# Modulation rows by column parts in the opening of an S4 convolution and SwiGLU kernel

## Chip, core and metric

The kernel runs on one core of a Trainium2 chip. The metric is the device time of one execution in microseconds, the median of several runs. TensorE (PE) multiplies, VectorE (DVE), ScalarE (ACT) and GpSimd (POOL) work on tiles of 128 partitions, SyncE (SP) issues transfers.

## Reference

```python
def _A_ref(u, A_re, A_im, B_re, B_im, C_re, C_im, log_dt, Dskip):
    dt = jnp.exp(log_dt)[:, None]
    ...
    P = jnp.exp(logdA[:, :, None] * l[None, None, :])
    K = jnp.einsum("dn,dnl,dn->dl", Cc, P, dB).real
    ...
    y = ... + u * Dskip[None, None, :]      # causal convolution of u with K, by FFT

def _B_ref(x, w_gate, w_up, w_down):
    g = _silu(x @ w_gate)
    u = x @ w_up
    return (g * u) @ w_down

x = A_u                                      # 1 x 2048 x 448
mod = (_silu(c) @ w_mod).reshape(c.shape[0], 6, 1, -1)
sa, ca, ga, sb, cb, gb = (mod[:, 0], mod[:, 1], mod[:, 2], mod[:, 3], mod[:, 4], mod[:, 5])
h = _layernorm(x, axis=-1) * (1 + ca) + sa
x = x + ga * _A_ref(h, ...)
h = _layernorm(x, axis=-1) * (1 + cb) + sb
x = x + gb * _B_ref(h, ...)                  # F = 1792
```

A condition vector c gives six rows of 448 values: a shift, a scale and a gate for each of two branches (groups 0 to 5 of `w_mod`). The first branch is a causal convolution over the 2048 tokens, the second a gated feed-forward.

## The kernel before

The 2048 tokens are 16 tiles of 128; blocks of 2, 2, 3, 3, 3 and 3 tiles pass through the feed-forward one after another (`run_blocks`). In a block, `gate_up` multiplies the block's transposed, normed rows by a column strip of both weights (line 703), split into a high and a low part (`hhi`, `hlo`, `gu`) so that one-pass products keep the precision; Silu (ACT, 718), a multiply (DVE, 731) and a split into `phi` and `plo` (734, 735) follow, and `down` multiplies the last strip but one by its down-weights (747). The next block's convolution and norm run between.

With the sizes of the states here the convolution kernel K is nearly linear in time, and the kernel takes it as K0 - slope, two rows `k0` and `k1`, if a flag that it computes allows it (`flag_sum`, `flag_of`; another path stands in the program otherwise). A convolution is then a product with a triangle of ones plus running sums of the tiles before (`run0`, `run1`).

The opening (lines 257 to 481) prepares all that for the first two tiles:

- SP loads states, x and the modulation weights in the order of `ORDER` ("sc": a state, "m10": group 1, first half, "w0": a strip of gate_up, "d0": of down, "x2": a tile of x).
- The steps run in the order of `PLAN`, a hand-set list of names out of the table `todo` (lines 434 to 481). Each engine executes its own instructions in this order, and each waits for what it needs.
- A modulation row (`mod_part`, 237 and 241): the columns of silu(c) are spread over 128 columns as the stationary operand, and five products sum in one bank, so that all 128 partitions hold the row: 1+ca and sa (groups 1, 0), the branch gate ga (group 2), 1+cb (4), sb (3), and gb (5, in two parts, `end_gate`).
- K's sums are columns (channel on the partition): `total` on ACT, `slope` on DVE. `row_of` (354) spreads such a column to a row in four products with the identity. The gate ga is then multiplied into `k0`, `k1` and the spread Dskip (`gd`).
- Convolution of the two tiles (437): `o00` to `o14`; the skip `hd` and x itself enter through products with the identity (322, 437).
- Norm (`st`, `r`, `n1`, `n2`), turning to channels (`to_channels`, 403), `hhi` and `hlo` (408, 413). The shift sb is added as a row ahead of the turn; as columns (`sbc`, for the later blocks) it is turned by line 373.
- The running rows after tile 1 come from three full and fast products with `left` (393) and go to partition 0 by `left_sbuf` (397).
- The weights of the first strips are split by ACT (116, 124) and DVE or POOL (118, 126, 128).

In the main loop the running rows are made on partitions 96 to 127, and a transfer that ACT issues brings the last of them to partition 0 (930 to 932).

Of the kernel before, what the change touches and what calls it, by code (L numbers as in the profile page):

```python
# [40 lines left out]
ORDER = """sf x0 x1 sc m10 se m11 sd m20 m21 m00 sb m01 sa m40 m41 d0 w0 m30 m31 m50 w2 d1 x2 w1 x3 d2 m51"""  # L41

PLAN = """t1 t4 pa0 t2 pa1 pg0 pg1 t3 S1 ca h00 S2 ps0 wr wi ps1 a2 m0 t5 a3 sq1 k0 cb0 S3 ga cb1 w0 h01 gd h11 m1 k1 gm0 h10
hd0 sb0 gm1 hd1 gc1 v00 v10 gc0 o00 o01 sq0 o02 o10 v01 sa w02 d10 o13 st0 r0 o12 cbr v11 d11 o11 o14 sb1 n10 w2 w01
st1 r1 d00 sbr e0 n11 n20 du0 tr0 n21 hi0 du1 tr1 l0 fs l1 sbt lo00 hi1 w1 lo10 fl lo01 sbc x1 e1 lo11 w11 w21 x0 eg
w22 lc w12 d01"""
# [6 lines left out]
def f32(ap):  # L53
    return ap.bitcast(F32)
# [3 lines left out]
def tile_kernel(ctx, tc, x, a_re, a_im, b_re, b_im, c_re, c_im, log_dt, dskip,  # L58
# [172 lines left out]
    cs = const.tile([128, 5], F32)  # L231

# [11 lines left out]
    def end_gate(ks):  # L244

        mod_part(CV, m5.rearrange("p a b -> p (a b)"), ks)
# [9 lines left out]
    with tc.tile_pool(name="pre", bufs=1) as pre:  # L256
        vec = pre.tile([128, 8], F32)
        sc.dma_start(vec, vecs)
        drow = pre.tile([1, D], F32)
        sc.dma_start(drow, dskip.rearrange("(o d) -> o d", o=1))  # L260
# [30 lines left out]
        all1 = pre.tile([128, 128], F32)  # L291
# [6 lines left out]


        left = pre.tile([128, 3, 33], F32R)  # L300
        left_ = pre.tile([128, 3, 33], F32)
        po.memset(left_, 0.0)
        po.memset(left_[:, 0, 0:1], 1.0)
        for q in range(2):
            po.memset(left_[:, 1 + q, 32:33], 1.0)
            po.tensor_scalar(left_[:, 1 + q, 0:1], tok, -1.0, 256.0 - 128.0 * q, op0=OP.mult, op1=OP.add)
        po.tensor_copy(left, left_)
# [13 lines left out]
        for q in range(2):  # L321
            pe.matmul(os[q], ident, xs[q], start=True, stop=False)
        pd = bank()[:, 0:D]
        pe.matmul(pd, all1[0:1, :], drow, start=True, stop=True)
        sc.copy(gd, pd)
# [11 lines left out]
                               (("h", F32, D), ("v0", F32, D), ("v1", F32R, D), ("hd", F32, D), ("h2", F32, 512)))  # L337
        sbr = pre.tile([128, 512], F32)
        ga = pre.tile([128, D], F32)
        t_, WV = f32(tri), po  # L340

        def part(t, k):
            return t[:, k * N:min((k + 1) * N, NS_)]
# [700 lines left out]
```

## Time and profile before

| | us |
|---|---|
| median of 3 runs | 490.55 (489.42 to 490.78) |
| the profiled execution | 488.68 |
| its span, first to last instruction | 486.9 |
| TensorE busy | 477.3 |
| DVE, ACT, POOL busy | 283.2, 155.0, 61.8 |
| start of line 703 | 38.64 |
| first product of line 747 | 43.81 |
| mean granted TensorE clock | 0.998 |

A row of a timeline gives the start from the span's first instruction, the time until the end of the last of the instructions that the row merges, the engine (a q behind it: its queue, which issues or waits), the line and operation, what it writes and reads, the shape and the number of records. A bracket gives idle time of the engine ahead of the row and what ended it. A full-precision product is shown as two records.

### The profile page before, as it was taken

What the parts mean: (1) busy time and instruction counts of PE and PEld (TensorE: products, weight loads), DVE (VectorE), ACT (ScalarE), POOL (GpSimd) and SP (SyncE); (2) the same over time, 40 slices, a digit from 0 to 9 for tenths busy, and PEclk for the clock granted to TensorE, in tenths of its full rate; (3) what the DMA queues carried; (4) which work ended last, traced back from release to release, by engine and by line L of the source; (5) the groups of instructions that cost most, each with busy time, mean ns of one, the idle gap of its engine ahead of it and who ended that gap; (6) DMA issues with size and microseconds to landing.
All of it is one profiled execution on the core that took longest, in us unless ns stands there. A gap on an engine that the chain in (4) does not pass through costs nothing.

```text
span 486.9 us, 6980 instructions
## 1 busy us (share of the span) xinstructions
PE 477.3 (98%) x2725; PEld 447.4 (92%) x2725; DVE 283.2 (58%) x543; ACT 155.0 (32%) x338; POOL 61.8 (13%) x86
## 2 busy tenths in 40 slices
PE   8999999999999999999999999999999999999994
PEld 5749988999998999999999999999999999999994
DVE  4868999568886446574644667375475643222134
ACT  5665455522225112332312223231223222221111
POOL 2241001000000040410023221002241000000000
PEclk9999999999999999999999999999999999999999
DMA  8945762020000200101210011130001112000001
GB/s 310 415 161 156 235 193 88 15 96 1 0 3 14 83 1 0 42 30 52 80 44 0 2 43 45 43 114 0 2 0 45 43 44 75 23 1 0 1 0 63
DMA packets 18751, 31.24 MB, mean 64 GB/s; under 512 B 2578, under 2 KB 13460, under 8 KB 18708
## 3 DMA queue, kind: packets, MB, share of 16 engines
q1 hardware_dynamic: 18000, 30.52, 18.3%
q8 instruction: 23, 0.38, 0.3%
q10 hardware_dynamic: 708, 0.19, 0.2%
q14 instruction: 20, 0.16, 0.1%
HBM read 24.61 MB, written 6.03 MB: 63 GB/s over the span
## 4 chain that ended last, share of the span: by engine, by line
PE 94%; DVE 2%; ACT 2%; issue 1%; POOL 0%; DVEq 0%; POOLq 0%; ACTq 0%
PE bank L703 57%; PE dn L747 27%; PE bank L237 2%; PE bank L253 1%; PE dn L437 1%; PE bank L241 1%; ACT raw L196 1%; PE bank L907 1%; PE cv L908 1%; PE cv L906 1%; PE cv L237 0%; PE bank L393 0%; DVE raw L194 0%; PE bank L207 0%; PE bank L920 0%
## 5 line engine op out<-in xcount | busy, mean ns | idle before, releaser
L703 PE MATMUL bank<-hhi,gu 128*128 128x384 f32 (+1 forms) x1169 | 209.4, 318 | 0.0
L703 PEld LDWEIGHTS bank<-hhi,gu 128*128 128x128 f32 x1169 | 189.8, 188 | 3.2 <-issue 0.7
L703 PE MATMUL bank<-hlo,gu 128*128 128x384 f32 (+1 forms) x668 | 130.8, 317 | 0.0
L703 PEld LDWEIGHTS bank<-hlo,gu 128*128 128x128 f32 x668 | 109.2, 188 | 0.0
L731 DVE TENSOR_TENSOR bank<-raw,bank 128x384 f32<-128x384 f32 (+1 forms) x69 | 36.8, 534 | 122.7 <-PE bank L703 120.3
L734 ACT CAST phi<-bank 128x384 fp32r<-128x384 f32 (+1 forms) x83 | 36.9, 445 | 140.8 <-DVE bank L731 140.8
L718 ACT ACTIVATE raw<-bank 128x384 f32<-128x384 f32 (+1 forms) x70 | 32.9, 470 | 121.8 <-PE bank L703 115.3
L735 DVE TENSOR_TENSOR plo<-bank,phi 128x384 fp32r<-128x384 f32 (+1 forms) x83 | 42.5, 512 | 37.6 <-ACT phi L734 37.6
L747 PE MATMUL dn<-wdh,plo 128*128 128x448 f32 x218 | 58.0, 367 | 0.0
L747 PE MATMUL dn<-wdh,phi 128*128 128x448 f32 x218 | 58.0, 367 | 0.0
L747 PE MATMUL dn<-wdl,phi 128*128 128x448 f32 x218 | 57.6, 365 | 0.0
L747 PEld LDWEIGHTS dn<-wdh,plo 128*128 128x128 f32 x218 | 41.0, 188 | 3.6
L747 PEld LDWEIGHTS dn<-wdl,phi 128*128 128x128 f32 x218 | 41.0, 188 | 3.5
L747 PEld LDWEIGHTS dn<-wdh,phi 128*128 128x128 f32 x218 | 38.7, 188 | 1.8 <-ACT run L930 0.7
L168 POOL TENSOR_SCALAR rsb<-mvb 128x1 f32<-128x1 f32 (+2 forms) x13 | 4.7, 360 | 170.6 <-DVE mvb L152 170.6
L168 POOL TENSOR_SCALAR rsa<-mva 128x3 f32<-128x3 f32 (+1 forms) x6 | 1.4, 233 | 118.1 <-DVE mva L152 118.1
L124 ACT CAST gu<-raw 128x1024 fp32r<-128x1024 f32 x14 | 14.6, 1046 | 0.3 <-ACT ga L379 0.3
L881 POOL TENSOR_TENSOR m<-m,gm 128x448 f32<-128x448 f32 x9 | 10.4, 1152 | 21.3 <-DVE m L185 21.3
L895 DVE TENSOR_TENSOR vl<-m,vh 128x448 fp32r<-128x448 f32 x12 | 9.1, 755 | 6.7 <-ACT vh L894 6.1
L237 PE MATMUL bank<-wm,cs 128*128 128x448 f32 x30 | 12.5, 546 | 0.0
L126 DVE TENSOR_TENSOR gu<-raw,gu 128x768 fp32r<-128x768 f32 x13 | 12.3, 950 | 0.0
L118 DVE TENSOR_TENSOR wdl<-rawd,wdh 128x448 fp32r<-128x448 f32 x16 | 9.9, 621 | 3.4 <-ACT wdh L116 3.2
(213 smaller groups left out, 417.8 us busy)
## 6 DMA issues: line engine op xcount, KB each, us to landing
raw<-in_B_w_gate_up_dram SPq DMA_DIRECT2D x14, 512.0 KB, 3.8
rawd<-in_B_w_down_dram SPq DMA_DIRECT2D x16, 224.0 KB, 3.9
x<-in_A_u_dram SPq DMA_DIRECT2D x12, 224.0 KB, 2.9
out_dram<-x SPq DMA_DIRECT2D x11, 224.0 KB, 2.4
xd<-raw SPq DMA_DIRECT2D x9, 256.0 KB, 2.0
raw<-xd SPq DMA_DIRECT2D x36, 64.0 KB, 2.0
wm<-in_w_mod_groups_dram SPq DMA_DIRECT2D x5, 448.0 KB, 8.0
wm<-in_w_mod_groups_dram SPq DMA_DIRECT2D x5, 336.0 KB, 7.9
```

Of the source, the lines that this page charges most:

```text
L118: ve.tensor_tensor(lo, wdn[j], f32(hi), op=OP.subtract)
L124: sc.copy(wgu[j][:, :, 0:4, :], w)
L126: en.tensor_tensor(lo, w[:, :, 0:3, :], f32(hi), op=OP.subtract)
L237: pe.matmul(ps[:, 0:D], cs[:, k:k + 1].to_broadcast([128, 128]), w[:, k * D:(k + 1) * D], start=k == 0, stop=False)
L703: pe.matmul(ps[s][:, 0:n], w[:, s, a], (hlo if lo else hhi)[:, k, 0:n], start=first and q == 0, stop=end and q == len(ka) - 1)
L718: sc.activation(p[:, 0:n], ps[0][:, 0:n], AF.Silu)
L731: ve.tensor_tensor(ps[1][:, 0:n], p[:, 0:n], ps[1][:, 0:n], op=OP.mult)
L734: sc.copy(hi[:, 0:n], ps[1][:, 0:n])
L735: ve.tensor_tensor(lo[:, 0:n], ps[1][:, 0:n], f32(hi[:, 0:n]), op=OP.subtract)
L747: pe.matmul(dn[q][:, 0:D], u[:, cs], v, start=f == 0 and z == 0, stop=f == (NF - 3 if last else NF - 1) and z == 2)
L881: (ve if on_v else po).tensor_tensor(v, h, g, op=OP.mult)
L895: ve.tensor_tensor(vl, v0, f32(vh), op=OP.subtract)
```

## The change

Four of the six modulation rows (groups 2, 4, 3 and 5) are no longer summed in one bank over all partitions. `mod_quads` writes each of the contraction's four parts to its own 32 partitions, with 32 columns of the stationary operand. ACT copies the bank to `qt`, and the sum over the four parts is taken in one of two ways: one product with `pick`, a column that has a one in the first row of each part and is spread over 128 columns (`spread_row`, for 1+cb and gb), or by turning `qt` to columns and summing on DVE (`turned_to`, `columns`, for ga and sb).

The branch gate is so a column `gac`. POOL multiplies it into K's column sums (`scaled`, `gated_dt`) and into Dskip, which now comes with the small vectors as columns (`gdm`) and is spread like K's sums (`gd_row`). Three row multiplies, the copy of the gate's row and its transfer leave the path taken here. sb is added as columns behind the turn (`high`, `low`). The last 64 channels, which need both halves of the partitions, are turned by two products of 64 columns.

Tile 1's x is added by POOL and DVE (`skip`, `branch_1`) in place of two products with the identity, and the running rows after tile 1 come from two fast products with ones into `CV`, a sum on DVE and a transfer that ACT issues (`left_over`, `left_rows`). The small splits of the first strip move from POOL to DVE, and both lists of order are written anew.

```diff
-ORDER = """sf x0 x1 sc m10 se m11 sd m20 m21 m00 sb m01 sa m40 m41 d0 w0 m30 m31 m50 w2 d1 x2 w1 x3 d2 m51"""
...
+ORDER = """sf x0 x1 sc m10 se sd m11 m20 m21 m00 sb m01 sa m40 m41 m30 m31 w0 m50 m51 d0 w1 d1 x2 w2 x3 d2"""
...
+    def mod_quads(ps, w):
+
+        for k in range(3):
+            pe.matmul(ps[32 * k:32 * k + 32, 0:D], cs[:, k:k + 1].to_broadcast([128, 32]), w[:, k * D:(k + 1) * D],
+                      start=True, stop=True)
+        for z in range(2):
+            pe.matmul(ps[96:128, z * D // 2:(z + 1) * D // 2], cs[:, 3 + z:4 + z].to_broadcast([128, 32]), w[:, 3 * D:NM],
+                      start=z == 0, stop=z == 1)
...
+        ve.memset(pick, 0.0)
+        for q in range(4):
+            ve.memset(pick[32 * q:32 * q + 1], 1.0)
...
-        for q in range(2):
-            pe.matmul(os[q], ident, xs[q], start=True, stop=False)
-        pd = bank()[:, 0:D]
-        pe.matmul(pd, all1[0:1, :], drow, start=True, stop=True)
-        sc.copy(gd, pd)
+        pe.matmul(os[0], ident, xs[0], start=True, stop=False)
...
+        def turned_to(ps, t):
+
             for k in range(4):
-                pe.transpose(psm["c"][:, k * 128:(k + 1) * 128], sbr[:, k * 128:(k + 1) * 128], ident)
...
+                o = ps[:, k * 128:(k + 1) * 128]
+                if k < 3:
+                    pe.transpose(o, t[:, k * 128:(k + 1) * 128], ident)
+                else:
+                    for z in range(2):
+                        pe.matmul(o[64 * z:64 * z + 64], t[:, 384:D], ident, start=True, stop=True)
+
+        def columns(to, n):
+            ve.tensor_reduce(to, psm[n].rearrange("p (k a b) -> p k a b", k=4, a=4)[:, :, :, 0], axis=AX.X, op=OP.add)
+
+        def spread_row(n):
+            pe.matmul(psm[n][:, 0:D], pick.to_broadcast([128, 128]), qt[n], start=True, stop=True)
+
+        def gd_row():
+            psm["d"] = bank()
+            row_of(gdm, psm["d"], ident[:, 0:64])
+
+        def scaled(o, a, b):
+            po.tensor_tensor(o, a, b, op=OP.add)
+            po.tensor_tensor(o, o, gac, op=OP.mult)
+
+        def gated_dt():
+            po.tensor_tensor(dt2, dt2, gac, op=OP.mult)
+            po.tensor_tensor(ndt2[:, 2:4], ndt2[:, 2:4], gac[:, 2:4], op=OP.mult)
+            po.tensor_tensor(a2[:, 0:2], a2[:, 0:2], gac[:, 0:2], op=OP.mult)
...
-            for k in ks:
-                u, w = ((f32(left[:, 0]), v0[k]) if k < 2 else (left[:, k - 1], v1[k - 2]))
-                pe.matmul(psm["l"][0:33, 0:D], u, w, start=k == 0, stop=k == 3)
...
+        def left_over():
+            for q in range(2):
+                pe.matmul(CV[:, 0:D], all1, v1[q], start=q == 0, stop=q == 1)
+
+        def left_rows(z):
+            e = slice(96, 128)
+            if z:
+                ve.tensor_tensor(run0[e], run1[e], os[1][e], op=OP.add)
+                sc.dma_start(run[0:1], run[127:128])
+            else:
+                sc.copy(run1[e], CV[e, 0:D])
...
+        def skip(q):
+            po.tensor_tensor(hd[q], hd[q], xs[q], op=OP.add)
+
+        def branch_1():
+            ve.tensor_tensor(xs[1], os[1], hd[1], op=OP.add)
...
-                sc.copy(hhi[:, k, c_], pk[k][:, c_])
...
+                sc.activation(hhi[:, k, c_], pk[q][:, k * 128:(k + 1) * 128], AF.Identity, bias=sbc[:, k:k + 1])
...
-                ve.tensor_tensor(hlo[:, k, c_], pk[k][:, c_], f32(hhi[:, k, c_]), op=OP.subtract)
...
+                ve.scalar_tensor_tensor(hlo[:, k, c_], pk[q][:, k * 128:(k + 1) * 128], sbc[:, k:k + 1], f32(hhi[:, k, c_]),
+                                        op0=OP.add, op1=OP.subtract)
```

How the lists of order move instructions shows at three places that the prediction speaks of. First TensorE in the middle of the opening, from the first modulation row to the rows of K; `wm` are modulation weights, `cs` the columns of silu(c). Before:

```order
L237 MATMUL bank<-wm_123,cs 128x448 x3
L241 MATMUL bank<-wm_123,cs 128x224 x2
L237 MATMUL bank<-wm_130,cs 128x448 x3
L241 MATMUL bank<-wm_130,cs 128x224 x2
L237 MATMUL bank<-wm_133,cs 128x448 x3
L241 MATMUL bank<-wm_133,cs 128x224 x2
L354 MATMUL cv<-ident,m_241 128x128 x3
L354 MATMUL cv<-ident_181,m_241 128x64
```

With the change:

```order
L238 MATMUL bank<-wm_123,cs 128x448 x3
L242 MATMUL bank<-wm_123,cs 128x224 x2
L248 MATMUL bank<-wm_130,cs 32x448 x3
L251 MATMUL bank<-wm_130,cs 32x224 x2
L238 MATMUL bank<-wm_133,cs 128x448 x2
L373 MATMUL bank<-ident,qtg 128x128 x3
L376 MATMUL bank<-ident,qtg 64x128 x2
L238 MATMUL bank<-wm_133,cs 128x448
L242 MATMUL bank<-wm_133,cs 128x224 x2
L352 MATMUL cv<-ident,m_233 128x128 x3
L352 MATMUL cv<-ident_181,m_233 128x64
```

The gate's row (wm_130) is by column parts now, and its turn stands inside the row of group 0 (wm_133), ahead of K's first row. Then TensorE at the end of the opening, up to the branch on the flag. Before:

```order
L403 MATMUL bank<-ident,h_0_257 128x128 x4
L403 MATMUL bank<-ident,h_1_258 128x128 x4
L393 MATMUL bank<-v_0_251,left 33x448
L393 MATMUL bank<-v_1_252,left 33x448
L426 MATMUL bank<-sz,ones 1x2
L393 MATMUL bank<-v_0_253,left 33x448
L393 MATMUL bank<-v_1_254,left 33x448
L373 MATMUL bank<-ident,sbr 128x128 x4
L237 MATMUL cv<-m_79,cs 128x448
L241 MATMUL cv<-m_79,cs 128x224 x2
L486 TENSOR_LOAD flag
```

With the change:

```order
L373 MATMUL bank<-ident,qts 128x128 x3
L376 MATMUL bank<-ident,qts 64x128 x2
L248 MATMUL bank<-m_79,cs 32x448 x3
L251 MATMUL bank<-m_79,cs 32x224 x2
L405 MATMUL cv<-v_0_245,all_178 128x448
L405 MATMUL cv<-v_1_246,all_178 128x448
L373 MATMUL bank<-ident,h_1_250 128x128 x3
L376 MATMUL bank<-ident,h_1_250 64x128 x2
L382 MATMUL bank<-qtb,pick 128x448
L506 TENSOR_LOAD flag
```

The last product ahead of the blocks is now the one that spreads gb (m_79 are group 5's weights), and it reads `qtb`, which ACT copies. Third, ACT at the same place. Before:

```order
L438 COPY h_1_258<-h_1_258 128x64
L408 CAST hhi<-bank 128x128 x4
L124 CAST gu_158<-raw 128x2x512
L376 COPY sbc<-bank 128x4
L473 COPY x_73<-dn_69 128x448
L473 COPY x_72<-dn_68 128x448
L438 COPY gb<-cv 128x448
L397 COPY run<-bank 1x448 x2
L486 TENSOR_LOAD flag
```

With the change:

```order
L428 ACTIVATE hhi<-bank,sbc 128x128 x4
L411 DMA run<-run 1x16x56
L469 COPY qtb<-bank 128x448
L455 COPY x_72<-dn_68 128x448
L455 COPY gb<-bank 128x448
L123 CAST gu_153<-raw 128x2x512
L115 CAST wdh_150<-rawd_81 128x448
L123 CAST gu_159<-raw 128x2x512
L115 CAST wdh_155<-rawd_82 128x448
L506 TENSOR_LOAD flag
```

The transfer of the running rows stands ahead of the copy of group 5's parts, and the splits of strips 1 and 2 and of their down-weights, which stood ahead of the copy of gb before, stand behind it.

More of the change, by code (lines that the diff above doesn't have):

```diff
@@ L231, in tile_kernel @@
     cs = const.tile([128, 5], F32)
+    pick = const.tile([128, 1], F32)
+    gac = const.tile([128, 4], F32)
     def mod_part(ps, w, ks):
@@ L290, in tile_kernel @@
         far = pre.tile([128, 128], F32R)
[L291 removed]
+        all1 = pre.tile([128, 128], F32R)
         ve.tensor_scalar(far, J, 128.0, None, op0=OP.add)
@@ L448, in tile_kernel @@
[L448 to L453 removed]
+            "m0": do(scaled, m0, m0, m0_), "m1": add(m1, a1, a2), "dg": gated_dt, "k0": do(row_of, m0, CV), "k1": do(row_of, m1, DN[2]),
```

125 lines of the change are left out of this document (50 added, 75 removed).

## The prediction

> **What bounds the kernel now.** I read the page first, then TensorE's timeline over the opening, then the other engines in that stretch.
>
> ```profile
> span 486.9 us, 6980 instructions
> PE 477.3 (98%) x2725; PEld 447.4 (92%) x2725; DVE 283.2 (58%) x543; ACT 155.0 (32%) x338; POOL 61.8 (13%) x86
> PE 94%; DVE 2%; ACT 2%; issue 1%; POOL 0%; DVEq 0%; POOLq 0%; ACTq 0%
> L168 POOL TENSOR_SCALAR rsb<-mvb 128x1 f32<-128x1 f32 (+2 forms) x13 | 4.7, 360 | 170.6 <-DVE mvb L152 170.6
> ```
>
> TensorE is busy for 98% of the span and is 94% of the chain of waits, so a change pays only if TensorE starts the blocks' work (line 703) sooner, or waits less behind that start. The diff rewrites the opening alone. TensorE there:
>
> ```profile
> 1.58 5.79 PE L253 MATMUL bank<-tri 128*128 128x512 f32 x14 [1.58 <-DVE tri L286]
> 7.21 1.66 PE L322 MATMUL dn<-x,ident 128*128 128x448 f32 x4
> 8.81 1.01 PE L324 MATMUL bank<-drow,all 1*128 1x448 f32 x2
> 9.75 2.52 PE L237 MATMUL bank<-wm,cs 128*128 128x448 f32 x6
> ...
> 12.87 2.42 PE L237 MATMUL bank<-wm,cs 128*128 128x448 f32 x6
> 15.12 0.92 PE L241 MATMUL bank<-wm,cs 128*128 128x224 f32 x4
> 15.88 2.42 PE L237 MATMUL bank<-wm,cs 128*128 128x448 f32 x6
> ...
> 22.79 1.00 PE L354 MATMUL dn<-ident,m 128*128 128x128 f32 x8
> 23.63 1.72 PE L237 MATMUL bank<-wm,cs 128*128 128x448 f32 x4
> 25.19 0.92 PE L437 MATMUL dn<-v,tri 128*128 128x448 f32 x2
> ...
> 29.57 0.91 PE L237 MATMUL bank<-wm,cs 128*128 128x448 f32 x2
> ...
> 34.68 1.69 PE L393 MATMUL bank<-v,left 128*33 128x448 f32 x4 [0.36 <-DVE hlo L413]
> 36.30 0.19 PE L426 MATMUL bank<-sz,ones 128*1 128x2 f32 x2
> 36.42 0.60 PE L393 MATMUL bank<-v,left 128*33 128x448 f32 x2
> 36.86 0.60 PE L373 MATMUL bank<-ident,sbr 128*128 128x128 f32 x4
> 37.29 0.92 PE L237 MATMUL cv<-m,cs 128*128 128x448 f32 x2
> ...
> 38.64 0.44 PE L703 MATMUL dn<-hhi,gu 128*128 128x256 f32 x1
> ...
> 43.81 0.57 PE L747 MATMUL dn<-wdh,phi 128*128 128x448 f32 x2
> ```
>
> Starts follow each other without a gap from 7.21 to 38.64, where line 703 begins; the first down-product (747) follows at 43.81. A full-precision product is two passes: three of 448 columns are six records and take 2.25 (12.87 to 15.12), so 0.75 each and 0.376 a pass; two of 224 take 0.76; a modulation row takes 3.01. A turn of 128 columns (373) takes 0.11. Where the array's shape changes it costs extra: the one-row product at 8.81 occupies 0.94, not 0.75, so two changes cost 0.19. Six rows at 3.01 are 18 of the 31 us.
>
> **The change, part by part, on TensorE.** I add up until the last turn of tile 1, then follow what stands behind it.
>
> First stage. The identity product of tile 1 (0.75) and the Dskip product (0.94) go. But the loads were exchanged: sd now stands ahead of the second half of group 1, which takes sd's landing.
>
> ```profile
> 4.49 0.65 SPq L266 DMA_DIRECT2D sd<-in_A_states_dram  x1
> sd<-in_A_states_dram SPq DMA_DIRECT2D x1, 448.0 KB, 6.9
> ```
>
> So it lands at 4.49 + 6.9 = 11.4; the third product waits there, and 0.75 + 0.76 end at 12.9, against 12.87 before. The two products are paid back as a wait. The loads that SP's queue now has later (the weights that stood ahead of groups 3 and 5) are not used before the opening's end. The branch gate now reaches the sums of K as columns: a column sum on DVE and a small product on POOL stand ahead of k0, covered by the second half of group 0's row (1.5); by POOL's nearest row, line 168 with 0.36, some 0.6 would show if that cover were gone.
>
> Q, a row by column parts: five products with 32 columns each. No row of before has products on different column parts beside each other. Upper end: one after another, 3.01, as the 33-column products show that narrow is not shorter by itself (34.68 to 36.30 is 1.62 for two). Lower end: all four parts together, the 0.75 of one. I take a value between: a product's two passes use the same columns and cannot overlap, and starts follow the program, so the second pass of one part can run with the first of the next only. That is four steps of 0.376 and two of 0.19, 1.88. With two changes of shape (0.19): Q = 2.07; ends 0.94 and 3.2.
>
> T, a turn by columns: three turns (0.33), two half-wide products of two passes of 0.11 (0.33 by the same overlap, ends 0.22 and 0.44), two changes: T = 0.85, ends 0.74 and 0.96.
>
> Second stage, to the first convolution product: before 12.87 to 25.19. After: one row 3.01, three spread rows k0, gd, k1 of 0.84 (22.79 to 23.63), the product with pick 0.75, and 2Q + T: 6.28 + 2Q + T. Third stage: before 4.38 (25.19 to 29.57); without tile 1's skip (0.75) 3.63. Fourth stage: the two full-precision line-393 products (1.62) go; flag 0.12 and two fast 448-column products 0.43 (36.42 to 36.86) stay; 0.55 + 2Q + 3T. Sum: 12.9 + 6.28 + 3.63 + 0.55 + 4 x 2.07 + 4 x 0.85 = **35.0** at the end of tile 1's turn.
>
> **What waits behind it.** Here the profile of the other engines speaks.
>
> ```profile
> 33.03 0.77 ACT L408 CAST hhi<-bank 128x128 fp32r<-128x128 f32 x4
> 36.78 0.86 DVE L413 TENSOR_TENSOR hlo<-bank,hhi 128x128 fp32r<-128x128 f32 x4
> 80.22 0.63 DVE L931 SCALAR_TENSOR_TENSOR run<-run,cv 32x448 f32<-32x448 f32 x1
> 80.88 0.50 ACTq L932 DMA_DIRECT2D run<-run  x1
> 81.43 0.57 ACT L116 CAST wdh<-rawd 128x448 fp32r<-128x448 f32 x1 [2.27 <-DVE run L931]
> 39.01 0.53 ACT L438 COPY gb<-cv 128x448 f32<-128x448 f32 x1 [0.48 <-PE cv L241]
> 34.71 1.07 ACT L124 CAST gu<-raw 128x1024 fp32r<-128x1024 f32 x1
> 37.57 1.81 DVE L126 TENSOR_TENSOR gu<-raw,gu 128x768 fp32r<-128x768 f32 x2
> 39.39 0.76 DVE L128 TENSOR_TENSOR gu<-raw,gu 64x256 fp32r<-64x256 f32 x2
> 40.19 0.63 DVE L118 TENSOR_TENSOR wdl<-rawd,wdh 128x448 fp32r<-128x448 f32 x1
> 41.61 0.43 DVE L731 TENSOR_TENSOR bank<-p,bank 128x256 f32<-128x256 f32 x1 [0.80 <-ACT p L718]
> 42.08 0.37 ACT L734 CAST phi<-bank 128x256 fp32r<-128x256 f32 x1 [0.57 <-DVE bank L731]
> ```
>
> The rows at 80 us show that ACT stands still until DVE's running row is done, issues the transfer in 0.50, and only then takes its next copy (idle 2.27). The change puts such a transfer ahead of the copy of the last gate row (qtb), and the product that spreads this row is TensorE's last ahead of line 703. Behind the waiting transfer stand qtb, x0, gb, the splits of gate_up 1 and 2 and the first Silu. So: hhi of tile 1 0.80, hlo 1.1 (DVE has a column added now; the row beside it is 0.86), running row 0.63, transfer 0.50, qtb 0.53, spread product 0.75, hand-overs 0.3: 4.6, and line 703 begins at **39.6**, 0.95 later than 38.64. TensorE stands idle for 3.8 of that.
>
> Behind it, from the end of the spread product: gb 0.53, ACT's split of gate_up 1 1.07, then DVE's splits, which stood beside TensorE's opening before and now stand behind this: 1.81 + 0.76 + two of line 118 (1.2) = 3.75, multiply 0.43, phi 0.37: 6.15. The first down-product comes at 45.75 against 43.81, **+1.94**. TensorE's own work would have had it there at 39.6 + 5.17 (38.64 to 43.81) = 44.8, so 1.0 is a new wait. From there on nothing differs. POOL's share of the splits moved to DVE is among these or ahead of it; the branch reads the flag earlier, which TensorE does not wait for.
>
> The profiled execution took 488.68 around its span of 486.9; + 1.94 is 490.6. It lies 1.87 below the median 490.55, against which runs are compared: forecast **492.5** (1.94 is 0.40%; I count under 0.3%, 1.5 us, as no change that a measurement can tell).
>
> **Rivals.**
> Column parts overlap fully (faster): Q = 0.94, T = 0.74 take 4 x 1.24 = 5.0 off TensorE. But then DVE is the bound.
>
> ```profile
> 29.77 0.63 DVE L151 BATCH_NORM_STATS2 stb<-dn 128x6 f32<-128x448 f32 x1 [0.18 <-PE dn L437]
> 30.65 0.68 DVE L416 SCALAR_TENSOR_TENSOR h<-dn,mvb,cbw 128x448 f32<-128x448 f32 x1
> ```
>
> The convolution ends at 12.9 + 6.28 + 2 x 0.94 + 0.74 + 3.63 = 25.4, or 26 with some waiting for loads. Behind it DVE has sum 0.63, statistics 0.8, flag 0.3, norm 0.68, a split of gate_up 0 0.95 and the column sum 0.2, 3.5 in all; then hhi 0.8, hlo 1.1, the other split 0.4, hlo 1.1, running row 0.63, transfer, copy and spread product 1.8, hand-overs 0.5: line 703 at 35.8, the down-product 6.15 later at 41.95, -1.9: **488.7**. For it: nothing shares columns. Against it: two passes per product. The Trainium skill, "TensorE: Matmul & The Clock Gate", section "Part 3: Packing small matmuls", states that matmuls on different column groups ran concurrently, three of 32 columns 2.38 times as fast. By that figure, as an estimate, Q would be 3.01 / 2.38 + 0.19 = 1.45 and the time about 490; no run here shows it, and the page does not say whether its products had two passes.
>
> Column parts do not overlap (slower): Q = 3.2, T = 0.96 add 4 x 1.24 = 5.0, all on TensorE's chain: +6.9, **497.5**. It decides from Q above about 2.4. For it: the 33-column rows show no gain; against it: they share their columns.
>
> The clock falls in the new idle (slower):
>
> ```profile
> 480.48 0.28 PE L775 MATMUL dn<-wdh,plo 128*128 128x192 f32 x1
> 482.00:487.00 5.00, 0.00 (x0) 0.00 (x0) 0.00 (x0) 0.00 (x0) 0.00 (x0) 0.75 0.27 86
> ```
>
> The last product ends at 480.76; a mean granted clock of 0.75 over 482 to 487 is half speed for the second half, so it fell some 3.7 us after, and the new idle is 3.8. At the kernel's start 14 one-pass products of 512 columns took 5.6, 0.40 each, where one of 448 takes 0.21 later (36.42 to 36.86): half speed for some 5 us. Here that loses 2.5, less the 1.0 of waiting that it covers: **494.0**. The Trainium skill, same page, section "Part 1: The HAM clock gate", puts the fall after an idle window of about 3.4 us; the trace agrees as far as it goes (3.7).
>
> That the transfer does not hold ACT (no change): hlo, running row and transfer would no longer stand ahead of qtb, and 1.1 + 0.63 + 0.50 = 2.2 would go from both starts: 490.3. The rows at 80 us speak against it.
>
> **How the numbers follow.** Half overlap 0.45 (slower 0.28, same 0.15, faster 0.02; in it the transfer that does not hold ACT; own range 490.6 to 494.4, from hand-overs and shape changes 0.1 each way at some 18 places); full overlap 0.30 (faster 0.25, same 0.05); none 0.18 (slower); clock 0.07 (slower). Faster 0.27, same 0.20, slower 0.53. The range holds the full case with 0.9 of error below it, and the serial case to a little above its middle: 487.8 to 497.8.
>
> **What would show it.** On TensorE's timeline: the five products of a row by column parts from first start to next row (1.9 half, 0.8 full, 3.0 none); the third product of group 1 at 11.4; an idle of 3 to 4 us ahead of the last pick product, ended by ACT's qtb copy, that one by the run transfer; line 703 at 39.6 and line 768 (747 before) at 45.7 with a wait of about 1.0 ended by ACT's phi. The granted clock below 1.00 in 38 to 45 us would show the fall. I am wrong if line 703 starts without that idle, if the opening is bound by DVE from the convolution on, or if time differs behind 50 us.

## The result, and the profile after

The change takes 492.0 us (median of 10 runs, 490.89 to 494.92) against 489.99 us for the kernel before (10 runs, 488.93 to 490.78): a ratio of 1.0055, 95% interval 1.0034 to 1.0076. It is slower by a little over half a per cent. The forecast was 492.5, slower. The time and its sign came out; two of the steps that lead there did not, as the profile shows.

The page of the changed kernel:

```profile
span 489.1 us, 7021 instructions
PE 475.3 (97%) x2743; PEld 447.7 (92%) x2743; DVE 284.2 (58%) x549; ACT 155.7 (32%) x336; POOL 62.3 (13%) x83
```

TensorE is busy for 2.0 us less than before in a span that is 2.2 us longer: work went, and idle time came. Where it came is in TensorE's timeline of the opening:

```profile
28.14 0.55 PE L373 MATMUL bank<-ident,qts 128*128 128x128 f32 x3
...
28.98 0.58 PE L248 MATMUL bank<-m,cs 128*32 128x448 f32 x3
...
29.87 0.68 PE L405 MATMUL cv<-v,all 128*128 128x448 f32 x2
30.93 0.55 PE L373 MATMUL bank<-ident,h 128*128 128x128 f32 x3 [0.37 <-ACT h L490]
31.40 0.44 PE L376 MATMUL bank<-ident,h 128*64 128x128 f32 x4
36.74 1.86 PE L382 MATMUL bank<-qtb,pick 128*128 128x448 f32 x2 [4.90 <-ACT qtb L469]
37.72 1.09 PE L724 MATMUL dn<-hhi,gu 128*128 128x256 f32 x1
...
45.10 0.67 PE L768 MATMUL dn<-wdh,phi 128*128 128x448 f32 x2
```

A row by column parts stands at 28.98, and the next kind of product starts at 29.87: all five products took 0.89, change of shape included; the third such row took 0.89 too (26.40 to 27.29), the second, with another shape behind it, 1.06 (18.87 to 19.93), and the first ends in a wait and can't be read so. A turn by columns took 0.84 (28.14 to 28.98). TensorE is done with tile 1's turn at 31.84, 3.2 us sooner than forecast. Then it stands for 4.90 us until ACT's copy of qtb. The spread product behind that takes 1.86, nearly twice the 1.02 that it takes at full clock in runs below, and from the start of line 724 to the first down-product 7.38 us pass, where 5.17 passed before. What ACT did meanwhile, with the rows of DVE and POOL that it waited for:

```profile
28.46 1.71 POOL L168 TENSOR_TENSOR rsb<-rsb,mhalf 128x1 f32<-128x1 f32 x1
30.20 0.67 ACT L490 ACTIVATE h<-h,rsb 128x448 f32<-128x448 f32 x1 [2.21 <-POOL rsb L168]
31.93 1.12 DVE L433 SCALAR_TENSOR_TENSOR hlo<-bank,sbc,hhi 128x128 fp32r<-128x128 f32 x4 [2.11 <-ACT hhi L428]
32.47 1.14 ACT L428 ACTIVATE hhi<-bank,sbc 128x128 fp32r<-128x128 f32 x4
34.80 0.63 DVE L410 TENSOR_TENSOR run<-run,dn 32x448 f32<-32x448 f32 x1
35.51 0.61 ACTq L411 DMA_DIRECT2D run<-run  x1
36.16 0.53 ACT L469 COPY qtb<-bank 128x448 f32<-128x448 f32 x1 [2.54 <-issue]
```

The transfer of the running row holds ACT as forecast: it waits for the sum on DVE (34.80), is issued at 35.51, and only then is qtb copied, though its bank had been ready since 30. The rows ahead of that show why the sum on DVE was no earlier. POOL's power for tile 1's norm (28.46 to 30.17) holds ACT's scaled rows of tile 1 (30.20) and with them, in ACT's queue, the high parts of both tiles; DVE stands for 2.11 until the first of these are there (31.93). Tile 1's high parts begin at 32.47, 0.63 after TensorE's turn of that tile, and take 1.14, not the 0.80 of the forecast: these two are nearly all of the 1.1 by which the idle is longer than the 3.8 that was forecast.

Short windows of the same trace show why the products behind it are slow; the third number from the right is the granted clock:

```profile
34.00:34.50 0.50, 0.00 (x0) 0.00 (x0) 0.50 (x3) 0.00 (x0) 0.00 (x0) 1.00 0.00 0
34.50:35.00 0.50, 0.00 (x0) 0.00 (x0) 0.47 (x3) 0.00 (x0) 0.00 (x0) 0.53 0.39 74
...
41.00:41.50 0.50, 0.50 (x4) 0.50 (x4) 0.47 (x2) 0.50 (x2) 0.00 (x0) 0.64 0.00 0
```

A mean of 0.53 puts the fall to half speed at 34.53, one of 0.64 the return at 41.36 (1.00 in the next window): the clock fell 2.7 us into the idle.

At the first down-product the change is 1.29 us late (45.10 against 43.81). That is not all. The stores at the ends of the first two blocks, of the kernel before and of the change:

```profile
100.36 1.54 SPq L810 DMA_DIRECT2D out_dram<-x  x2
157.01 1.54 SPq L810 DMA_DIRECT2D out_dram<-x  x2
```
```profile
102.60 1.54 SPq L831 DMA_DIRECT2D out_dram<-x  x2
160.49 1.54 SPq L831 DMA_DIRECT2D out_dram<-x  x2
```

The lag is 2.24 at the first and 3.48 at the second, in code that the diff does not touch. It stays there (3.73 at the last product), and 1.5 come back behind the last product, where the program's end takes 4.6 us instead of 6.1. So 1.3 + 2.2 + 0.3 - 1.5 = 2.2 between the spans. The 2.2 between 45 and 160 us are in the products of 256 columns. From one group of eleven (seven with hhi, four with hlo) to what follows, in the kernel before and in the change:

```profile
113.66 0.96 PE L703 MATMUL bank<-hhi,gu 128*128 128x256 f32 x7
...
114.91 0.57 PE L747 MATMUL dn<-wdh,phi 128*128 128x448 f32 x2
```
```profile
112.61 0.99 PE L724 MATMUL bank<-hhi,gu 128*128 128x256 f32 x7
...
113.91 0.57 PE L768 MATMUL dn<-wdh,phi 128*128 128x448 f32 x2
```

1.25 us became 1.30, at a granted clock of 1.00 in both. The blocks of two tiles have 616 such products, 56 groups; 0.05 on each would be 2.8 us. Some groups of the kernel before take 1.30 as well, as is shown further on.

So three things were to be found out: what a row by column parts costs, what the idle and its clock cost apart, and why untouched products became slower.

### The profile page after: what moved, and what is told of

It is laid out like the page before. It is cut to its first block, busy times and chain, and to the rows that moved or that the text cites. A ratio compares the mean times of both kernels' runs of the same rounds, so it can differ in the third digit from the quotient of the medians.

```text
span 489.1 us, 7021 instructions
## 1 busy us (share of the span) xinstructions
PE 475.3 (97%) x2743; PEld 447.7 (92%) x2743; DVE 284.2 (58%) x549; ACT 155.7 (32%) x336; POOL 62.3 (13%) x83
## 4 chain that ended last, share of the span: by engine, by line
PE 88%; DVE 2%; ACT 2%; issue 1%; ACTq 0%; DVEq 0%
PE bank L724 58%; PE dn L768 27%; ACT raw L195 1%; PE bank L928 1%; PE cv L927 0%; PE cv L929 0%; DVE raw L193 0%; PE dn L724 0%; PE bank L206 0%; PE bank L941 0%; PE bank L382 0%; DVE x L807 0%; ACT raw L194 0%; PE cv L942 0%; PE cv L940 0%
## 5 line engine op out<-in xcount | busy, mean ns | idle before, releaser
L724 PE MATMUL bank<-hhi,gu 128*128 128x384 f32 (+1 forms) x1169 | 212.3, 320 | 0.0
L724 PEld LDWEIGHTS bank<-hhi,gu 128*128 128x128 f32 x1169 | 192.1, 189 | 3.5 <-issue 1.1
L125 DVE TENSOR_TENSOR gu<-raw,gu 128x768 fp32r<-128x768 f32 x14 | 13.3, 951 | 4.7 <-ACT gu L123 4.7
L194 ACT ACTIVATE raw<-raw,rsb 128x64 f32<-128x64 f32 x14 | 4.8, 346 | 21.0 <-DVE raw L193 11.9
```

Source lines behind the costliest of these rows:

```text
L125: en.tensor_tensor(lo, w[:, :, 0:3, :], f32(hi), op=OP.subtract)
L724: pe.matmul(ps[s][:, 0:n], w[:, s, a], (hlo if lo else hhi)[:, k, 0:n], start=first and q == 0, stop=end and q == len(ka) - 1)
```

## The experiments

Twelve kernels ran, each beside the kernel before on the same chip. Ratios are to that kernel, with 95% intervals. The first four rows are from one chip, the next four from a second, the last four from a third; the kernel before took 489.14, 489.35 and 488.34 there, so rows of different chips are compared by their ratios.

| kernel | median, us | ratio |
|---|---|---|
| transfer_late | 488.70 | 0.9995 (0.9984 to 1.0006) |
| clock_held | 491.55 | 1.0055 (1.0042 to 1.0068) |
| one_column_part | 498.72 | 1.0200 (1.0185 to 1.0216) |
| gate_row_first | 486.28 | 0.9945 (0.9933 to 0.9957) |
| change_again | 491.86 | 1.0058 (1.0042 to 1.0073) |
| old_addresses | 490.09 | 1.0014 (1.0004 to 1.0024) |
| before_moved_64 | 490.83 | 1.0039 (1.0025 to 1.0054) |
| gate_row_first_old_addresses | 484.67 | 0.9916 (0.9899 to 0.9933) |
| flag_later | 484.54 | 0.9921 (0.9908 to 0.9935) |
| splits_ahead | 484.24 | 0.9916 (0.9902 to 0.9929) |
| splits_ahead_256 | 484.23 | 0.9910 (0.9897 to 0.9923) |
| gate_up_256_alone | 487.58 | 0.9980 (0.9969 to 0.9992) |

**The same parts on one set of columns.**

```diff
         for k in range(3):
-            pe.matmul(ps[32 * k:32 * k + 32, 0:D], cs[:, k:k + 1].to_broadcast([128, 32]), ..., start=True, stop=True)
+            pe.matmul(ps[0:32, 0:D], cs[:, k:k + 1].to_broadcast([128, 32]), ..., start=k == 0, stop=False)
         for z in range(2):
-            pe.matmul(ps[96:128, ...], ..., start=z == 0, stop=z == 1)
+            pe.matmul(ps[0:32, ...], ..., start=False, stop=z == 1)
...
+        for n in "gcsb":
+            po.memset(qt[n], 0.0)
```

ACT's copies to `qt` take 32 rows in place of 128.

> The five products of a row by column parts all go to the first 32 columns, one after another into one sum; the other 96 rows are zeros, so what follows is the same. Theory A (parts on different columns overlap fully, so a row costs 0.9 to 1.1 now): each row takes 3.0, the four add 4 x 2.0 = 8.0 on TensorE; the last turn ends near 39.5 instead of 31.8, and with ACT's wait behind it line 724 begins 6 to 8 us later, the median rises by 5 to 8 us against the change. Theory B (half overlap, 1.9 to 2.1 a row, as was forecast): each row takes 1.0 more, the four add 4, and the median rises by 2.5 to 4. Theory C (no overlap): within 1 us of the change.

TensorE's timeline of this kernel, at its third such row:

```profile
30.96 2.42 PE L248 MATMUL bank<-wm,cs 128*32 128x448 f32 x6
...
34.07 0.55 PE L375 MATMUL bank<-ident,h 128*128 128x128 f32 x3
```

3.11 a row (30.96 to 34.07) against 0.89, and the median is 6.9 us above that of the change (498.72 against 491.86, ratios 1.0200 and 1.0058). Theory A holds, the half overlap and no overlap fall. The width of the products is the same in both kernels, and so are their two passes; what differs is the columns, and with them that the parts now sum in one place of the bank. No run keeps one of these two and changes the other. The Trainium skill, "TensorE: Matmul & The Clock Gate", section "Part 3: Packing small matmuls", gives 2.38 times for three products of 32 columns on different column groups; here four groups gave 2.9 to 3.5 times at two passes a product (3.11 against 1.06 and 0.89), so the page holds in kind; its figure is for three groups, and no run here has three.

**The idle ahead of the last spread product.** The transfer alone moved to the end of the opening's list:

```diff
-... hi1 lo1 lr1 gqc x0 gbk gb w1 w11 w12 d00 d01 w2 w21 w22 d10 d11"""
+... hi1 lo1 lr1 gqc x0 gbk gb w1 w11 w12 d00 d01 w2 w21 w22 d10 d11 lrd"""
...
                 ve.tensor_tensor(run0[e], run1[e], os[1][e], op=OP.add)
-                sc.dma_start(run[0:1], run[127:128])
...
+            "lrd": lambda: sc.dma_start(run[0:1], run[127:128]),
```

> Only the running row's transfer moves, from its place ahead of the copy of qtb on ACT to the end of ACT's opening. Theory A (TensorE's idle of 4.90 us ahead of the last spread product is made by ACT's queue, which stands from 33.6 to 36.1 for this transfer, and the clock falls in that idle): qtb is copied at 33.6, the spread product starts near 34.2, the idle is 2.4 us, too short for the fall, so the granted clock stays at 1.00; line 724 begins near 34.9 instead of 37.72 and the first down-product some 6.2 us later, at 41 instead of 45.10; the median falls by about 4 us against the change, 2 below the kernel before (ratio 0.996). Theory B (other waits end at the same time anyway, tile 1's low parts or the splits on DVE): the idle shrinks but the first down-product stays within 0.5 of 45.1 and the median within 1 us of the change's.

The spread product and the first down-product of this kernel:

```profile
35.15 1.02 PE L382 MATMUL bank<-qtb,pick 128*128 128x448 f32 x2 [2.24 <-ACT qtb L468]
...
42.67 0.66 PE L767 MATMUL dn<-wdh,phi 128*128 128x448 f32 x2 [1.19 <-ACT phi L754]
```

The idle is 2.24, the granted clock is 1.00 throughout, the spread product takes its usual time, and the median is 3 us below the change's (488.70, ratio 0.9995 against 1.0055; 4 us and a ratio of 0.996 were expected). Theory A holds for the place; the first down-product came at 42.67 and not at 41, since the opening of this run was 1 us later than in the first profile of the change, and since it now waits 1.19 for phi, with DVE's splits ahead of the multiply.

**The clock apart from the idle.** Eighteen fast products that nothing reads fill the idle, and every wait stays:

```diff
-... hi1 lo1 lr1 gqc x0 gbk gb ...
+... hi1 lo1 lr1 fill gqc x0 gbk gb ...
...
+        def fill(n):
+            for _ in range(n):
+                pe.matmul(DN[2].rearrange("p (a b) -> p a b", a=4), tri, tri[:, None, :].to_broadcast([128, 4, 128]),
+                          start=True, stop=True)
```

> 18 fast products of 512 columns into a bank that nothing reads go into TensorE's idle ahead of the last spread product; every wait stays as it is. They are work added that no result uses. Theory A (the granted clock falls in the idle and costs time by itself): the clock stays at 1.00, the spread product takes 0.95 instead of 1.86, line 724 has its full pace at once, and the first down-product comes about 1.0 us earlier than 45.10 (bound then by DVE's splits behind the copy of gb, not by TensorE, which could be there at 42.8); the median falls by 1 to 2 us against the change. Theory B (the low granted clock covers only work that waits anyway): within 0.5 us of the change.

> The change as it is, beside the others on one chip. Theory A: as before, first products of 256 columns 119 ns apart in the first two blocks, ratio 1.004 to 1.007; it sets the level against which the run with the filler products is read, and tells whether the 1 us by which the later kernels' opening lagged in the first profile of the change (its first turn of tile 0 at 27.3 us, theirs at 28.1 to 28.4) belongs to the run: then this profile may have it anywhere between 27 and 28.5.

The filler, the spread product and the first down-product with the clock held, and then the spread product of the change run once more:

```profile
32.79 4.39 PE L421 MATMUL dn<-tri 128*128 128x512 f32 x18
37.77 1.02 PE L382 MATMUL bank<-qtb,pick 128*128 128x448 f32 x2 [0.59 <-ACT qtb L474]
...
45.29 0.68 PE L773 MATMUL dn<-wdh,phi 128*128 128x448 f32 x2 [1.17 <-ACT phi L760]
```
```profile
37.64 1.86 PE L382 MATMUL bank<-qtb,pick 128*128 128x448 f32 x2 [4.90 <-ACT qtb L469]
```

With the clock held, 7.52 us pass from the start of the spread product to the first down-product; in the change run once more 8.55 (to 46.19), in its first profile 8.36. So the half-speed clock costs 0.8 to 1.0 us there: the products lose more (the last group ahead of the first down-product starts 7.73 after the spread product in the change's first profile, 44.47, and 5.71 with the clock held, 43.48), and the wait for phi of 1.17, which comes into view as soon as they are fast, hides the rest. The medians do not tell it: 1.0055 and 1.0058, with intervals of 0.0013 and 0.0016 to each side. By the traces the idle costs the larger part of the 3 us of transfer_late, the clock the smaller. The repeat also shows that the first profile's opening was an early one (it is of the fastest of its ten executions, 490.89): its first product of group 1's second half had its load at 10.77, the repeat's at 11.66. Against the kernel before, the repeat's first down-product is 2.38 late, not 1.29. The opening with the clock held was late too, which is why its first down-product came at 45.29 and not 1.0 ahead of 45.10.

**The gate row ahead of tile 1.** The transfer goes last as in transfer_late, and the copy of qtb, its spread product and the split of gate_up 1 go into ACT's and DVE's idle:

```diff
-tr0 xn1 sbt w01 sbc gq l1 hi0 tr1 lo0 lr0 w02 hi1 lo1 lr1 gqc x0 gbk gb w1 w11 w12 d00 d01 w2 w21 w22 d10 d11"""
+tr0 sbt w1 w01 sbc gq gqc xn1 l1 hi0 w11 w12 gbk tr1 lo0 hi1 lr0 w02 lo1 lr1 gb x0 d00 d01 w2 w21 w22 d10 d11 lrd"""
```

> The transfer goes to the end of ACT's opening as in the run before, the copy of qtb goes ahead of tile 1's normalised rows and its spread product ahead of tile 1's turn, and gate_up 1 is split in ACT's and DVE's idle ahead of tile 0's parts (28 to 31 us). Theory A (line 724 waits for this queue order alone): TensorE waits only for tile 1's high parts, line 724 begins near 33.5, its first stage takes 5.2 with DVE's splits hidden, the first down-product comes near 39 instead of 43.81 before and 45.10 in the change; the median falls to 485 to 486, ratio to the kernel before 0.990 to 0.992. Theory B (the branch, the weights' loads or DVE hold the start): line 724 begins after 36 and the median is not below 488.

```profile
33.69 0.36 PE L723 MATMUL dn<-hhi,gu 128*128 128x256 f32 x1 [0.56 <-ACT hhi L427]
...
40.29 0.68 PE L767 MATMUL dn<-wdh,phi 128*128 128x448 f32 x2 [1.05 <-ACT phi L754]
```

These rows of its TensorE timeline show the first gate_up product 5 us ahead of the kernel before (33.69 against 38.64), held only by tile 1's high parts, as theory A says. The first down-product is 3.5 us ahead and not 4.8: 1.05 of the gain turns into a wait for phi. The median (486.28, ratio 0.9945) stays above the 485 to 486 (0.990 to 0.992) that were expected.

**Why untouched products became slower.** The two new constants, pick and gac, take 32 bytes each in SBUF ahead of everything that is placed later. The split weights, phi and plo so begin at 288 modulo 512 bytes, where they began at 224 (the low down-weights at 32, where they began at 480); hhi and hlo lie where they lay. Taking the 64 bytes back in the change, and adding 64 unused bytes to the kernel before:

```diff
-    mhalf = const.tile([128, 1], F32)
...
-    pick = const.tile([128, 1], F32)
-    gac = const.tile([128, 4], F32)
+    bits = const.tile([128, 8], F32)
+    mhalf, pick, gac = bits[:, 0:1], bits[:, 1:2], bits[:, 2:6]
```
```diff
     cs = const.tile([128, 5], F32)
+    pads = [const.tile([128, 4], F32, name=f"pad{q}") for q in range(2)]
...
+        for q in range(2):
+            po.memset(pads[q], 0.0)
```

> The change with pick and gac in spare bytes of the tile of the constant -0.5, so that the two new constants no longer push all weights, phi and plo 64 bytes up in SBUF: they begin again at 224 modulo 512 bytes, as in the kernel before, and not at 288. Nothing else differs. Theory A (the 256-column products of the first two blocks are slower in the change, 119 ns apart against 113 to 115, because of where the weights lie): the step returns to 113 to 115, the 2.2 us that the change loses between the first down-product and the end of block 2 (45 to 160 us) are gone, and the median is 2.0 to 2.5 us below the change's. Theory B (the step comes from the chip, the run or the instructions' place in memory): 119 stays, within 0.5 us of the change.

> The kernel before with two unused constants of 32 bytes each, which push the weights, phi and plo 64 bytes up, to 288 modulo 512 as in the change. Theory A (addresses): the 256-column products step at 119 ns instead of 113 to 115, and the time rises by 2.0 to 2.5 us, ratio 1.004 to 1.005, with not one line of the opening changed. Theory B (not the addresses): the step stays at 113 to 115 and the ratio within 0.001 of 1.

> The order with the gate row first (486.28 us, ratio 0.9945) and the weights at the old addresses. Theory A (addresses): another 2.0 to 2.5 us go, ratio 0.989 to 0.991. Theory B: ratio 0.994 to 0.995.

Two groups of eleven in the second block, of the change with old addresses and of the kernel before moved by 64 bytes:

```profile
112.02 0.97 PE L723 MATMUL bank<-hhi,gu 128*128 128x256 f32 x7
...
113.28 0.96 PE L723 MATMUL bank<-hhi,gu 128*128 128x256 f32 x7
```
```profile
114.27 0.99 PE L706 MATMUL bank<-hhi,gu 128*128 128x256 f32 x7
...
115.57 1.00 PE L706 MATMUL bank<-hhi,gu 128*128 128x256 f32 x7
```

1.26 us with the old addresses, 1.30 in the kernel before once it is moved. It works in both directions: the change gets 1.8 us faster (490.09 against 491.86), the kernel before 0.39% slower with its opening unchanged, and the gate row first some 1.4 faster (ratio 0.9916 against 0.9945, on two chips). From the profiles, in us:

| kernel | weights at, mod 512 | first block | second block |
|---|---|---|---|
| before | 224 | 56.55 | 56.65 |
| before_moved_64 | 288 | 57.41 | 57.89 |
| change_again | 288 | 57.40 | 57.88 |
| old_addresses | 224 | 57.33 | 56.84 |
| gate_row_first | 288 | 57.50 | 57.90 |
| gate_row_first_old_addresses | 224 | 56.64 | 56.65 |

(First block: first down-product to its stores; second: from these to its own.) The expected 2.0 to 2.5 were 1.4 to 1.8 by medians and ratios, and in the change the first block did not come back.

The single groups show more than these sums. At 288, in the profiles of seven kernels (the change and its repeat, before_moved_64, transfer_late, clock_held, one_column_part, gate_row_first), no group of the first two blocks takes less than 1.30. At 224 both lengths occur, in stretches: the kernel before takes 1.25 to 1.26 from 45 to 70 us and 1.29 to 1.30 from 80 to 94, and old_addresses 1.29 to 1.30 from 47 to 107 (a little more where other products stand ahead). One such group of the kernel before, then one of old_addresses:

```profile
85.71 0.99 PE L703 MATMUL bank<-hhi,gu 128*128 128x256 f32 x7
...
87.01 0.58 PE L747 MATMUL dn<-wdh,phi 128*128 128x448 f32 x2
```
```profile
51.33 0.99 PE L723 MATMUL bank<-hhi,gu 128*128 128x256 f32 x7
...
52.63 0.99 PE L723 MATMUL bank<-hhi,gu 128*128 128x256 f32 x7
```

The granted clock is 1.00 there, and the weights lie at the same place modulo 512 as in the fast stretches. So in these runs the short step never occurs at 288, while the old place allows it without ensuring it. What decides between the two at 224, and so why the first block of old_addresses stayed slow, is open.

**Three steps further.** The flag made later; then the down weights' splits out of DVE's queue ahead of the multiply; then everything moved by 32 bytes, to 256 modulo 512.

```diff
-... st1 fl r1 n11 gc1 spc
-tr0 sbt w1 w01 sbc gq gqc xn1 l1 hi0 w11 w12 gbk tr1 lo0 hi1 ...
+... st1 r1 n11 gc1 spc
+tr0 sbt w1 w01 sbc fl gq xn1 gqc l1 hi0 w11 w12 tr1 gbk lo0 hi1 ...
```

> The gate row first with the old addresses (ratio 0.9916), and in the order the flag made only after tile 1's normalisation and the turned shift, with tile 1's scaled rows ahead of the copy of qtb. Theory A (POOL's power for tile 1 takes 1.71 instead of 0.57 because POOL reads the flag and branches beside it): that power takes 0.57, tile 1's rows, its high parts and line 724 come 0.7 to 1.1 earlier, the median falls by 0.5 to 1. Theory B (the 1.71 is a matter of POOL's power itself, 0.57 to 1.4 in the kernel before): it stays above 1.2 and the time within 0.3 us.

POOL's two instructions for tile 1 in that kernel:

```profile
29.30 0.71 POOL L167 TENSOR_SCALAR rsb<-mvb 128x1 f32<-128x1 f32 x1 [1.76 <-DVE mvb L151]
30.10 1.13 POOL L168 TENSOR_TENSOR rsb<-rsb,bits 128x1 f32<-128x1 f32 x1
```

They end 1.93 us after the first began (31.23); in gate_row_first_old_addresses, with the flag beside them, it was 2.01 (0.22 and 1.71, and the gap between). Theory A falls: the power alone is shorter, the instruction ahead of it longer by as much, and the flag does not slow the pair. The time is the same within its interval.

```diff
-tr0 sbt w1 w01 ... w11 w12 tr1 gbk ... gb x0 d00 d01 w2 w21 w22 d10 d11 lrd"""
+tr0 sbt d00 w1 w01 ... w11 w12 d01 tr1 gbk ... gb x0 w2 w21 w22 lrd"""
...
-                if fresh and f > 1:
+                if fresh and f > 0:
                     split_d(f)
```

> As the run before it, and the split of the first down weights ahead of TensorE's start (in DVE's idle), that of the second one block step later. Theory A (the wait of 1.16 us ahead of the first down-product is DVE's queue of splits ahead of the multiply): two splits of 0.62 leave that queue, the wait is gone or below 0.2, the median falls by another 0.8 to 1.2. Theory B (ACT's or the loads' side holds phi): the wait stays above 0.8.

```profile
39.23 0.67 PE L766 MATMUL dn<-wdh,phi 128*128 128x448 f32 x2 [0.24 <-ACT phi L753]
```

The wait, 0.73 in flag_later, went to 0.24, nearly as theory A says of the place. The first down-product went from 40.39 to 39.23, but at most 0.59 of that is the splits': this profile's opening was early, and line 722 began at 33.23 and not at 33.80. The median moved by 0.3 (484.24 against 484.54), which is within the intervals, not by 0.8 to 1.2; 0.4 us are left at the last product of the profile (477.21 against 477.62).

```diff
     cs = const.tile([128, 5], F32)
+    pad = const.tile([128, 4], F32)
...
+        po.memset(pad, 0.0)
```

> The run before it, with one unused constant of 32 bytes that moves the weights, phi and plo from 224 to 256 modulo 512 bytes. If the step of the 256-column products goes by whether the weights begin on a multiple of 128 or 256 bytes, it falls below 113 ns here and the time with it, by up to 2 us; if any move from 224 costs what 64 bytes cost, it is 119 and the time rises by 1.5 to 2.2; if 288 alone is bad, nothing changes (within 0.5 us).

> The run with everything at 256 modulo 512 had a shorter step for the 384-column products (173.4 ns against 175.1) and a longer one for the 448-column down-products (205.9 against 203.8). Here an unused gap of 224 bytes moves phi and plo (the fixed operand of the down-products) from 256 to 480, which is 224 modulo 256 as before, while the gate_up weights stay at 256. Theory A (the step of a product goes by the address of the operand that is loaded as weights): the 448-column step returns to 203.8 or less, the 384-column one stays at 173.4, and the median falls by 1 to 1.5 us below 484.2, ratio 0.988 to 0.989. Theory B (it goes by the moving operand, the down weights, which stay at 256): 205.9 stays and the time is within 0.5 us.

In the last of these an unused tile of 224 bytes at the head of the working tiles is added to it; so the working rows of the later convolutions and p, the output of Silu, move along with phi and plo. The blocks of three tiles, at 224, at 256, and at 256 with the gap (eleven products of 384 columns, then nine down-products):

```profile
303.47 1.40 PE L722 MATMUL bank<-hhi,gu 128*128 128x384 f32 x7
...
305.42 0.77 PE L766 MATMUL dn<-wdh,phi 128*128 128x448 f32 x3
...
307.24 1.39 PE L722 MATMUL bank<-hhi,gu 128*128 128x384 f32 x7
```
```profile
304.59 1.38 PE L724 MATMUL bank<-hhi,gu 128*128 128x384 f32 x7
...
306.50 0.78 PE L768 MATMUL dn<-wdh,phi 128*128 128x448 f32 x3
...
308.35 0.86 PE L724 MATMUL bank<-hhi,gu 128*128 128x384 f32 x4
```
```profile
302.32 0.77 PE L768 MATMUL dn<-wdh,phi 128*128 128x448 f32 x3
...
304.17 1.40 PE L724 MATMUL bank<-hhi,gu 128*128 128x384 f32 x7
...
306.11 1.40 PE L724 MATMUL bank<-hhi,gu 128*128 128x384 f32 x7
```

The rows of the kernel at 224 show one length of two: its 384-column groups take 1.91 to 1.95, its nine down-products 1.82 to 1.86, by stretches. At 256 the 384-column group is 1.90 to 1.92 throughout, the down-products are mostly 1.85 to 1.86, and the groups of 256 columns in the first two blocks take 1.29 to 1.31, about as at 288. Of the outcomes that were named for splits_ahead_256 the step is so that of the second (118 to 119 ns), and the time that of the third (484.23 against 484.24). With the gap the 384-column groups are nearly all at 1.94 to 1.95 and the down-products stay at 1.85: 3.3 us lost (487.58), and 0.03 us on each of the 112 groups of 384 columns is 3.4. Neither theory holds. The gate_up products read none of the tiles that the gap moves, and yet they became slower. So a product's step does not go by the address of its own weights alone; what it collides with stays open.

## Why the forecast was right, and where it was not

**What was right.** TensorE's start on the blocks and its waits behind it set the time of the opening. The turn by columns was put at 0.85 and took 0.84. The transfer of the running row holds ACT's queue and with it qtb, shown by transfer_late, which gave back 3 us. The first down-product was forecast at 45.75 and came at 45.10 and 46.19 in two profiles.

**The step that failed first is Q**, "a product's two passes use the same columns and cannot overlap, and starts follow the program": 2.07 was forecast, 0.89 to 1.06 measured, the lower end. Products on different columns run beside each other with both passes, as one_column_part shows with 3.11 for the same products on the same columns. The rival of full overlap had this, and that TensorE then no longer sets the end of the opening; it put line 724 at 35.8 and the median at 488.7. Line 724 came at 37.72. That rival's sum runs along DVE without a wait; in the trace DVE stands for 2.11 ahead of the first low parts, behind POOL's power and ACT's rows, and POOL has no term in the sum. It had neither the clock nor the addresses either. The clock makes up only 0.2 of line 724's delay: from the spread product's start to line 724's, 0.98 pass in the change and 0.77 (37.77 to 38.54) with the clock held.

**The clock's fall** stood among the rivals at 0.07, since the idle was put at 3.8 and the fall at 3.7 after the last product. The idle was 4.90, the fall came after 2.7 in the first profile and after 3.5 in the repeat (32.74 to 36.22). Its price was put at 1.5 (2.5 less 1.0 covered), and is 0.8 to 1.0.

**"From there on nothing differs"** was wrong. The prediction named a difference behind 50 us as a sign that it would be wrong, and that sign is there: 2.2 us in the profiles of the first two blocks. By the ratios 0.0044 of the 0.0058 by which the change is slower goes with the addresses (0.0014 is left), some 2 of 2.8 us. The diff shows two small constants; that they move every weight can be read there, but no row of the trace before could price it.

**So the number holds by errors of opposite sign.** In the first profile TensorE was done with tile 1's turn 3.2 us ahead of the forecast, since the rows were 1.0 to 1.2 cheaper each, less what waits for loads took back. The idle ate 1.05 more than forecast and the spread product at half speed 0.2, so line 724 began 1.9 early; 7.38 instead of 6.15 passed from there to the first down-product (6.75 with the clock held, 38.54 to 45.29), and 0.65 early was left. The repeat's opening was 0.9 later and came out 0.44 late. Where without the move of the weights the change would have been 0.14% slower (old_addresses), it was 0.58%. That the sum of these lands within 0.5 us of the forecast median is luck; that the change is slower rests in the larger part on the addresses, which the forecast did not have. Not explained is the program's end: 4.5 to 4.7 us from the last product in the profiles of the change and its variants, 6.1 and 5.2 in the two of the kernel before.

**A version that beats both.** gate_row_first_old_addresses takes 484.67 us, 0.84% less than the kernel before (0.9899 to 0.9933); the two steps behind it are no different within their intervals. The change as a whole was worth making: it was the order behind the column parts, and 64 bytes, that gave the gain away. What the column parts alone are worth against full rows in that order, no run shows.

## What to carry to other kernels

When a change makes the bounding engine faster, list for each of its remaining waits what stands ahead of the awaited instruction in its own engine's queue: a transfer that ACT issues, and that had to wait for DVE, held all that ACT had behind it here. A long idle of TensorE can cost more than itself: behind those of 4.90 and 4.31 us here the products ran at half speed, behind one of 2.24 they did not. And a new small constant moves all that is placed after it: compare the addresses, and the step of an untouched loop, before a difference is put down to the change.

## What was not expected of the hardware

- Five full-precision products on four sets of 32 columns took 0.89 to 1.06 us, 3.11 on one set.
- The half-speed clock lasted 6.83 us in the change (34.53 to 41.36, from the windows above) and 3.42 in one_column_part, from these two windows of its trace (half speed for 0.04 of the first, full speed for 0.12 of the second: 44.46 to 47.88):

```profile
44.00:44.50 0.50, 0.00 (x0) 0.00 (x0) 0.00 (x0) 0.50 (x2) 0.00 (x0) 0.96 0.00 0
...
47.50:48.00 0.50, 0.50 (x5) 0.50 (x4) 0.01 (x1) 0.50 (x2) 0.00 (x0) 0.62 0.00 0
```

- That is two times and one time 3.42. It fell 2.7 us after TensorE's last product in the one and 4.2 after it in the other (40.27). The Trainium skill, "TensorE: Matmul & The Clock Gate", section "Part 1: The HAM clock gate", states a free-running window of 3413 ns; the lengths agree, and a fall after only 2.7 us of idle shows that an idle need not last a whole window.
- Fast products of 256 columns have two steps some 4% apart at full clock (eleven in 1.25 to 1.26 us or in 1.29 to 1.31). With the weights at 224 modulo 512 bytes both occur, in stretches; 64 bytes further only the longer one does.
